# An attention and MLP-mixer kernel: sums transposed by TensorE, transposing DMAs two head pairs ahead, one store for 128 partitions, and another order in the first group's last token mixing

## The chip, the cores and the metric

The kernel runs on one core of one Trainium2 chip. The metric is the device time of one execution in microseconds (us). Before the change the median of three runs is 425.3 us (421.85 to 425.76).

## The reference, cut to what matters

The inputs are q, k and v of 8 batches, 12 heads, 448 positions and 64 elements a head, and four weight matrices. All is float32 outside; the kernel computes in fp16 with fp32 sums.

```python
scores = scale * q @ k.T - log(448)              # per batch and head, 448 x 448
attn   = 1 / (1 + exp(-scores))                  # a sigmoid, no softmax
x      = concat over heads of attn @ v           # 8 x 448 x 768
h      = relu(x.T @ w_tok1) @ w_tok2             # token mixing, 448 -> 256 -> 448
u      = x + h.T
h2     = relu(u @ w_ch1) @ w_ch2                 # channel mixing, 768 -> 1536 -> 768
out    = u + h2
```

## The kernel before, in words

The eight batches are four **groups** of two; the two batches of a group share the 128 partitions (64 each). A position is p * 7 + j, so a tile of 448 positions is seven blocks j of 64 partitions. Heads go in six **pairs** a group, 24 pairs in all, counted n = 6 * group + i.

Per pair, `load` (line 72) fetches k, q and v with six DMAs from the POOL queue, which turn fp32 into fp16. `turn` (line 96) makes kT and qT: in the first group TensorE transposes into PSUM and DVE copies out; later, DVE copies k and q into an order that suits (line 106, tiles kp and qp) and SP issues one transposing DMA each (line 109). `scores(i, j)` (line 135) makes four matmuls and a sigmoid on ACT; `values(i)` (line 158) makes 28 matmuls into xT; `back(i)` (line 180) turns xT into x_nat, by TensorE in the first group and by a transposing DMA later.

Token mixing is `tok1` (lines 202 to 217, tiles k1 and h1T) and `tok2(j)` (lines 219 to 250): DVE adds PSUM to x_nat and writes u in fp32, and then DVE or ACT casts u to u16 in fp16. `uturn(j)` (line 252) turns u16 into uT: in the first group TensorE transposes and DVE or ACT copies out, in the later groups SP issues a transposing DMA a block (line 255). Channel mixing is `ch1` (line 275: six matmuls of 512 or 384 columns, then a relu on DVE into h2aT) and `ch2` (line 293: twelve matmuls of 384 columns, then a DVE add into u), followed by `store(j)`: two DMAs from SP, one for each half of the partitions.

Nothing is scheduled by a planner: the order is the order in which the code is written. `first_attention` writes the first group's attention with the first two thirds of its token mixing between the rounds, and the last third (columns 512 to 768) behind it. `phase(grp, nxt)` then writes 38 units of the channel mixing of one group: 12 of `ch1` on blocks 0 to 3, 12 on blocks 4 to 6, and 14 of `ch2`. Among the first 30 it puts the attention of the next group in visits of three rounds, the first visit behind the second unit; among the last eight it puts that group's token mixing (`front1`, `front2`). PSUM has three double banks ("pair", used by scores, values and token mixing) and two single ones ("one"). Each engine takes its instructions in order, and so do the queues of SP and POOL.

In the trace and below, names lose part of their numbers: qk_1_0 in the second group is the score tile of pair i = 1 and block j = 0, c_0_6_0 is unit 6 of `ch1` of group 0 on blocks 0 to 3 (or a tile of `ch2`, where line 297 says so), xb is the tile of `back`, yn that of `tok2`, ut that of `uturn`, tk and tq those of `turn` in the first group.

## Time and profile before

| | |
|---|---|
| median of three runs | 425.3 us (421.85 to 425.76) |
| profiled execution | 417.46 us, of which the span is 415.7 us |
| PE busy | 372.6 us, 90% of the span, 3348 matmuls |
| DVE, ACT, POOL busy | 169.1, 190.3 and 92.9 us |
| chain that ended last | PE 70%, DMA 16%, DVE 7%, POOL 3% |
| mean granted TensorE clock | 0.97 |
| DMA, of the time of 16 engines | 39.9% POOL's queue, 38.0% SP's queue |

A share of busy time is a mean over stages. The groups are worked on one after the other: the first group's attention fills the span up to about 62 us, its last token mixing up to 72 us, and then come four phases that begin at about 72, 170, 267 and 356 us. Idle time of PE inside these stretches is what the views of waits and windows show. A matmul's own duration includes a part that overlaps the next one, so that a series is priced by its whole time or by the distance from start to start.

### The profile page before, as it was taken

How to read it: one execution, taken by the hardware profiler on the slowest of the kernel's cores; microseconds unless marked ns; L12 is line 12 of the kernel's file. 1: busy time of each engine (PE TensorE's matmuls, PEld its weight loads, DVE VectorE, ACT ScalarE, POOL GpSimd, SP SyncE). 2: the span in 40 equal slices, each digit the busy share in tenths (PEclk: the TensorE clock that was granted, in tenths of full speed). 3: DMA queues.
4: the chain of work that ended last, by engine and by line, in shares of the span. 5: the costliest groups of instructions: out<-in, count | busy, mean ns of one | idle time of the engine just before them, and what ended most of it. 6: DMA issues, size and time to landing. Idle time of an engine off the chain costs nothing.

```text
span 415.7 us, 8015 instructions
## 1 busy us (share of the span) xinstructions
PE 372.6 (90%) x3348; PEld 191.6 (46%) x3348; DVE 169.1 (41%) x310; ACT 190.3 (46%) x214; POOL 92.9 (22%) x159
## 2 busy tenths in 40 slices
PE   2988977949799999949799999979999999999995
PEld 1444544414355555414355455424555555446662
DVE  1258673313342117822432224843432118655231
ACT  2896834537676630246766821067778530000000
POOL 8796344321422200231513300030000000000000
PEclk9999997769999999978999999999999999999999
DMA  7999999993999944995999963792543517500233
GB/s 104 182 194 182 196 128 197 165 150 52 143 135 160 149 123 92 172 145 85 111 156 116 142 166 77 147 176 46 113 59 70 118 43 127 122 0 2 76 92 99
DMA packets 96532, 49.98 MB, mean 120 GB/s; under 512 B 70256, under 2 KB 92784, under 8 KB 96496
## 3 DMA queue, kind: packets, MB, share of 16 engines
q0 software_dynamic: 25104, 21.93, 39.9%
q1 hardware_dynamic: 71392, 27.54, 38.0%
q8 instruction: 26, 0.43, 0.5%
q14 instruction: 10, 0.08, 0.1%
HBM read 43.84 MB, written 11.01 MB: 132 GB/s over the span
## 4 chain that ended last, share of the span: by engine, by line
PE 70%; DMA 16%; DVE 7%; POOL 3%; issue 2%; ACT 1%; POOLq 0%
DMA q_1_500<-in_q_dram 3%; DMA qT_1295<-qp_1296 2%; DMA qT_2455<-qp_2456 2%; DMA qT_2691<-qp_2692 2%; DMA qT_1535<-qp_1536 2%; DMA qT_3611<-qp_3612 2%; DMA k_5_239<-in_k_dram 1%; DMA k_1_86<-in_k_dram 1%; DMA uT_4409<-u_3_3_4417 1%; PE c_0_0_0_1271 L278 1%; PE c_0_6_0_1424 L278 1%; PE c_1_6_0_2580 L278 1%; PE c_0_1_0_1279 L278 1%; PE c_2_2_1_4360 L297 0%; PE c_2_2_0_4332 L297 0%
## 5 line engine op out<-in xcount | busy, mean ns | idle before, releaser
L278 PEld LDWEIGHTS <-w_ch_t 128*128 128x128 f16 x576 | 54.8, 100 | 63.6 <-issue 20.7
L297 PEld LDWEIGHTS <-h2aT_1269 128*128 128x128 f16 x168 | 15.5, 98 | 13.0 <-issue 3.5
L297 PEld LDWEIGHTS <-h2aT_3589 128*128 128x128 f16 x168 | 15.5, 98 | 13.0 <-issue 3.5
L297 PEld LDWEIGHTS <-h2aT_2433 128*128 128x128 f16 x168 | 15.5, 98 | 13.0 <-issue 3.5
L297 PEld LDWEIGHTS <-h2aT_4692 128*128 128x128 f16 x168 | 16.4, 98 | 10.9
L234 PEld LDWEIGHTS <-w_tok_n 128*64 128x64 f16 x252 | 13.0, 111 | 13.0 <-issue 8.6
L206 PEld LDWEIGHTS <-w_tok_t 64*128 64x128 f16 x252 | 12.5, 97 | 9.5 <-issue 3.0
L150 ACT ACTIVATE attn_0_0_3625<-qk_0_0_3624,att_bias 128x896 f16<-128x896 f32 x1 | 1.0, 1007 | 18.4 <-PE qk_0_0_3624 L143 18.4
L86 POOL DMA_DIRECT2D k_5_3615<-in_k_dram x2 | 1.2, 602 | 36.0 <-DVE qp_3612 L106 36.0
L86 POOL DMA_DIRECT2D k_5_2459<-in_k_dram x2 | 1.2, 602 | 35.0 <-DVE qp_2456 L106 35.0
L150 ACT ACTIVATE attn_0_0_2469<-qk_0_0_2468,att_bias 128x896 f16<-128x896 f32 x1 | 1.0, 1007 | 17.4 <-PE qk_0_0_2468 L143 17.4
L117 PE MATMUL tk_135<-ident,k_0_72 128*64 128x128 f16 x14 | 1.0, 311 | 5.6 <-POOL ident masks.py:199 5.6
L143 PE MATMUL qk_1_0_2566<-qT_2455,kT_2451 64*64 64x448 f16 x4 | 0.6, 570 | 5.4 <-DMA qT_2455<-qp_2456 5.4
L143 PE MATMUL qk_1_0_1410<-qT_1295,kT_1291 64*64 64x448 f16 x4 | 0.6, 571 | 5.3 <-DMA qT_1295<-qp_1296 5.3
L150 ACT ACTIVATE attn_0_0_178<-qk_0_0_177,att_bias 128x896 f16<-128x896 f32 x1 | 1.0, 1007 | 7.0 <-PE qk_0_0_177 L143 7.0
L285 DVE TENSOR_SCALAR h2aT_1269<-c_0_6_0_1424 128x512 f16<-128x512 f32 x1 | 0.7, 692 | 8.0 <-PE c_0_6_0_1424 L278 8.0
L285 DVE TENSOR_SCALAR h2aT_2433<-c_1_6_0_2580 128x512 f16<-128x512 f32 x1 | 0.7, 692 | 7.9 <-PE c_1_6_0_2580 L278 7.9
L143 PEld LDWEIGHTS <-kT_2451 64*64 64x64 f16 x28 | 0.8, 113 | 6.7 <-issue 6.5
L143 PEld LDWEIGHTS <-kT_1291 64*64 64x64 f16 x28 | 0.8, 113 | 6.6 <-issue 6.4
L86 POOL DMA_DIRECT2D k_5_1299<-in_k_dram x2 | 1.2, 609 | 11.5 <-DVE qp_1296 L106 11.5
L117 PEld LDWEIGHTS <-k_0_72 128*64 128x64 f16 x14 | 0.8, 165 | 5.5 <-issue 5.5
L150 ACT ACTIVATE attn_1_0_2567<-qk_1_0_2566,att_bias 128x896 f16<-128x896 f32 x1 | 1.0, 1007 | 5.0 <-PE qk_1_0_2566 L143 5.0
(1244 smaller groups left out, 954.0 us busy)
## 6 DMA issues: line engine op xcount, KB each, us to landing
w_ch_t<-in_moe_w_ch_dram POOLq DMA_DIRECT2D x6, 768.0 KB, 11.8
w_tok_t<-in_moe_w_tok_dram POOLq DMA_DIRECT2D x2, 224.0 KB, 6.1
out_dram<-u_0_120 SPq DMA_DIRECT2D x2, 192.0 KB, 2.9
out_dram<-u_1_122 SPq DMA_DIRECT2D x2, 192.0 KB, 7.8
out_dram<-u_2_124 SPq DMA_DIRECT2D x2, 192.0 KB, 4.1
out_dram<-u_3_126 SPq DMA_DIRECT2D x2, 192.0 KB, 2.6
out_dram<-u_4_128 SPq DMA_DIRECT2D x2, 192.0 KB, 2.7
out_dram<-u_5_130 SPq DMA_DIRECT2D x2, 192.0 KB, 3.2
```

The costliest lines, as they stand in the source:

```text
L86: nc.gpsimd.dma_start(out=t[64 * b : 64 * b + 64, :, :, :], in_=src[2 * g + b, 2 * i : 2 * i + 2].rearrange("h (p j) e -> p h j e", j=J),)
L117: nc.tensor.transpose(out=ps[64 * h : 64 * h + 64, j, :, :], in_=raw[:, h, j, :], identity=ident[:, :],)
L143: nc.tensor.matmul(out=ps[64 * b : 64 * b + 64, h, 0:S], lhsT=kT[64 * h : 64 * h + 64, j, b, :], rhs=qT[64 * h : 64 * h + 64, :, b, :], st ...
L150: nc.scalar.activation(out=at[:, :, :], in_=ps[:, :, 0:S], func=SIGMOID, bias=bias_t[:, :], scale=att_scale,)
L206: nc.tensor.matmul(out=ps[:, b, 0 : c1 - c0], lhsT=w_tok1_t[64 * b : 64 * b + 64, j, 128 * tcb : 128 * tcb + 128], rhs=self.x_nat[64 * b : ...
L234: nc.tensor.matmul(out=d[64 * b : 64 * b + 64, :], lhsT=w_tok2_n[:, tcb, j, :], rhs=self.h1T[:, b, tcb, c0 + w * m : c0 + w * m + w], star ...
L278: nc.tensor.matmul(out=ps[:, :, :], lhsT=w_ch1_t[:, db, 128 * cb : 128 * cb + 128], rhs=self.uT[:, db, j0:j1, :], start=(db == 0), stop=(d ...
L285: nc.vector.tensor_scalar(out=self.h2aT[:, cb, j0:j1, :], in0=ps[:, :, :], scalar1=0.0, scalar2=None, op0=MAX,)
L297: nc.tensor.matmul(out=ps[:, :], lhsT=self.h2aT[:, cb, j, :], rhs=w_ch2_t[:, cb, c], start=(cb == 0), stop=(cb == NCB - 1),)
```

## The change

1. **Two pairs ahead.** `turn(n)` for the pairs of the later groups is called at round (i, 3) for pair i + 2, where before it was round (i, 0) for pair i + 1. The second group's first two pairs are turned behind the first group's last `tok2` and before the third unit of the phase. `load` is now called through `load_to`, three pairs ahead of a turn and not four, v has seven buffers in place of six, `w_ch1` is loaded some rounds later, and the identity is made before the first loads.
2. **Sums transposed by TensorE.** `uturn` of the later groups makes six transposes a block on TensorE into a double bank, two blocks at a time, and ACT copies them out. The `front2` calls come one unit earlier, with the transposes one or two units behind them and the last block's behind the next phase's first unit.
3. **128-partition stores.** One DMA a block in place of two.
4. **fp16 sums first.** `tok2_late` in the first group's last token mixing lets DVE write u16 straight from PSUM; `rest` makes the same adds into the fp32 sums later. In the first phase the first two relus go to ACT.

```diff
     def load(n):
-        if n >= NG * NP:
-            return
...
-                bufs=6 if what == "v" else 8,
+                bufs=7 if what == "v" else 8,
...
         if "q" in whats:
-            load(n + 4)
+            load_to(n + 3)
...
-        def uturn(self, j, d0=0, d1=6, eng=None):
-            u16 = self.u16s[j]
-            if not self.first:
-                nc.sync.dma_start_transpose(out=self.uT[:, :, j, :], in_=u16[:, :])
-                return
-            ps = bank(f"ut_{self.g}_{j}_{d0}", [128, NDB, 128], FP16)
...
+        def tok2_late(self, js, c0, c1):
...
+            for m, j in enumerate(js):
+                nc.vector.tensor_tensor(
+                    out=self.u16s[j][:, c0:c1],
+                    in0=self.x_nat[:, j, c0:c1],
+                    in1=ps[:, m, 0:w],
+                    op=ADD,
+                )
+            def rest():
...
+            return rest
+        def uturn(self, j, d0=0, d1=6, eng=nc.scalar, nj=1):
+            n = d1 - d0
+            name = f"ut_{self.g}_{j}_{d0}"
+            if n == NDB:
+                ps = pp.tile([128, 2, 8, 128], FP16, tag="pair", bufs=3, name=name)
+            else:
+                ps = bank(name, [128, nj, n, 128], FP16)
+            for m in range(nj):
+                for db in range(n):
+                    c = 128 * (d0 + db)
+                    nc.tensor.transpose(
+                        out=ps[:, m, db, :],
+                        in_=self.u16s[j + m][:, c : c + 128],
+                        identity=ident[:, :],
+                    )
...
         def store(self, j):
-            for b in range(2):
-                nc.sync.dma_start(
-                    out=out[2 * self.g + b].rearrange("(p j) d -> p j d", j=J)[:, j, :],
-                    in_=self.us[j][64 * b : 64 * b + 64, :],
-                )
+            rows = out.rearrange("b (p j) d -> (b p) j d", j=J)
+            nc.sync.dma_start(
+                out=rows[128 * self.g : 128 * self.g + 128, j, :], in_=self.us[j][:, :]
+            )
...
-        if j == 0 and (i == NP - 1 or not grp.first):
-            turn(grp.g * NP + i + 1)
+        if j == 3 and not grp.first:
+            turn(grp.g * NP + i + 2)
...
-        for j in range(J):
-            grp.tok2(j, *cols, nc.scalar)
-            if j >= 2:
-                grp.uturn(j - 2, 4, 6, nc.scalar)
+        late = [grp.tok2_late(js, *cols) for js in ((0, 1), (2, 3))]
+        grp.uturn(0, 4, 6, nc.scalar, 2)
+        late.append(grp.tok2_late((4, 5), *cols))
+        grp.uturn(2, 4, 6, nc.scalar, 2)
+        late[0]()
+        grp.tok2_late((6,), *cols)()
+        turn(NP)
+        for f in late[1:]:
+            f()
...
+            if grp.first and f is units[2][1]:
+                turn(NP + 1)
             f()
...
-            4: lambda: front2((0, 1)),
-            5: lambda: front2((2, 3)),
-            6: lambda: front2((4, 5)),
-            7: lambda: front2((6,)),
+            3: lambda: front2((0, 1)),
+            4: lambda: front2((2, 3)),
+            5: lambda: (nxt.uturn(0, nj=2), front2((4, 5))),
+            6: lambda: (nxt.uturn(2, nj=2), front2((6,))),
+            7: lambda: nxt.uturn(4, nj=2),
```

The first place where the order moves is DVE at the end of the first group's last token mixing (u_0_0 to u_0_6 are the fp16 sums, u_0 to u_6 the fp32 ones, kp and qp the copies of `turn`). Before:

```order
L215 TENSOR_SCALAR h1T_118<-k_0_1_512_1184 128x2x256
L241 TENSOR_TENSOR u_0_120<-x_nat_117,yn_0_512_1200 128x256
L241 TENSOR_TENSOR u_6_132<-x_nat_117,yn_6_512_1258 128x256
L285 TENSOR_SCALAR h2aT_1269<-c_0_0_0_1271 128x512
L285 TENSOR_SCALAR h2aT_1269<-c_0_1_0_1279 128x512
L106 COPY kp_1292<-k_1_497 128x2x7x64
L106 COPY qp_1296<-q_1_500 128x2x7x64
```

The rows for u_1 to u_5 are left out there. After:

```order
L220 TENSOR_SCALAR h1T_118<-k_0_1_512_1158 128x2x256
L273 TENSOR_TENSOR u_0_0_121<-x_nat_117,yl_0_1174 128x256
L273 TENSOR_TENSOR u_0_5_131<-x_nat_117,yl_4_1202 128x256
L282 TENSOR_TENSOR u_0_120<-x_nat_117,yl_0_1174 128x256
L282 TENSOR_TENSOR u_1_122<-x_nat_117,yl_0_1174 128x256
L273 TENSOR_TENSOR u_0_6_133<-x_nat_117,yl_6_1221 128x256
L282 TENSOR_TENSOR u_6_132<-x_nat_117,yl_6_1221 128x256
L111 COPY kp_1229<-k_0_485 128x2x7x64
L111 COPY qp_1233<-q_0_488 128x2x7x64
```

The rows for blocks 1 to 4 are left out. Ten adds now stand between the relu of h1T and the copies of the second group's pair 0, and those copies, which stood in round (5, 0) of the first group's attention before, now stand here.

The second place is the queue of SP at the end of the second group's token mixing and the start of the third group's attention. Before:

```order
L309 DMA out_dram<-u_5_130 64x768 x2
L255 DMA_TRANSPOSE uT_2150<-u_1_5_2162 128x6x128
L309 DMA out_dram<-u_6_132 64x768 x2
L255 DMA_TRANSPOSE uT_2150<-u_1_6_2164 128x6x128
L109 DMA_TRANSPOSE kT_2451<-kp_2452 128x7x128
L109 DMA_TRANSPOSE qT_2455<-qp_2456 128x7x128
```

After:

```order
L350 DMA out_dram<-u_5_130 128x768
L350 DMA out_dram<-u_6_132 128x768
L114 DMA_TRANSPOSE kT_2523<-kp_2524 128x7x128
L114 DMA_TRANSPOSE qT_2527<-qp_2528 128x7x128
```

All seven transposing DMAs of the sums are gone. kT_2451 is the third group's pair 1 and kT_2523 is its pair 2: pairs 0 and 1 were issued in the group before.

## Rows read from the trace of the kernel before

**Rows 1.** The page: the TensorE clock granted, in 40 slices of the span.

```profile
PEclk9999997769999999978999999999999999999999
```

**Rows 2.** What PE waited for: us in total, times, longest us.

```profile
PE qk_1_0_2566 L143 <- DMA qT_2455<-qp_2456: 5.4, 1, 5.4
PE qk_1_0_1410 L143 <- DMA qT_1295<-qp_1296: 5.3, 1, 5.3
PE qk_3_0_2834 L143 <- DMA qT_2691<-qp_2692: 3.1, 1, 3.1
PE qk_3_0_1678 L143 <- DMA qT_1535<-qp_1536: 2.6, 1, 2.6
PE qk_1_0_3713 L143 <- DMA qT_3611<-qp_3612: 2.5, 1, 2.5
PE c_2_0_0_3591 L278 <- DVE u_6_2163 L305: 1.0, 1, 1.0
PE tk_192 L117 <- DMA k_1_86<-in_k_dram: 0.9, 1, 0.9
...
PE c_3_0_0_4693 L278 <- DMA uT_4409<-u_3_3_4417: 0.5, 1, 0.5
```

**Rows 3.** Windows: stretch, us, busy of PE, PEld, DVE, ACT, POOL, clock, DMA, GB/s.

```profile
72.10:77.30 5.20, 5.18 (x18) 1.92 (x21) 0.74 (x2) 0.69 (x2) 0.00 (x0) 0.54 1.16 210
...
89.90:95.00 5.10, 5.10 (x20) 1.63 (x20) 0.69 (x1) 1.90 (x2) 0.00 (x0) 0.60 1.09 139
```

**Rows 4.** The chain that ended last, second group's attention: start us, us, what.

```profile
90.81 2.68 PE c_0_6_0_1424 L278 x6
...
96.91 1.40 PE c_0_8_0_1486 L278 x6
```

**Rows 5.** Timeline, last token mixing and first visit: start us, us, engine, what.

```profile
65.48 0.69 DVE L215 TENSOR_SCALAR h1T_118<-k_0_1_512_1184 128x512 f16<-128x512 f32 x1 [2.80 <-PE k_0_1_512_1184 L206]
...
66.69 0.42 DVE L241 TENSOR_TENSOR u_0_120<-x_nat_117,yn_0_512_1200 128x256 f32<-128x256 f16 x1 [0.52 <-PE yn_0_512_1200 L234]
67.03 0.42 DVE L241 TENSOR_TENSOR u_1_122<-x_nat_117,yn_1_512_1207 128x256 f32<-128x256 f16 x1
...
72.12 2.72 PE L278 MATMUL c_0_0_0_1271<-uT_119,w_ch_t 128*128 128x512 f16 x6
...
77.26 0.38 PE L143 MATMUL qk_0_0_1308<-qT_930,kT_926 64*64 64x448 f16 x4
...
77.86 0.38 DVE L106 COPY kp_1292<-k_1_497 128x896 f16<-128x896 f16 x1
...
78.34 1.23 SPq L109 DMA_TRANSPOSE kT_1291<-kp_1292  x1
```

**Rows 6.** DMA issues: what, queue, count, us from issue to landing.

```profile
qT_1295<-qp_1296 SPq DMA_TRANSPOSE x1, 10.1
...
qT_3133<-qp_3134 SPq DMA_TRANSPOSE x1, 8.2
...
qT_3611<-qp_3612 SPq DMA_TRANSPOSE x1, 7.1
...
qT_3709<-qp_3710 SPq DMA_TRANSPOSE x1, 2.9
```

**Rows 7.** Timeline: seven transposes of 128 columns on TensorE, in `back`.

```profile
61.46 0.55 PE L189 MATMUL xb_5_1159<-ident,xT_5_1138 128*128 128x128 f16 x7
```

**Rows 8.** Line 189, the same transposes: duration ns min/median/max, first and last start.

```profile
L189 PE MATMUL xb_5_1159<-ident,xT_5_1138 x7: 216/218/219, 61.5 to 61.8; 128*128 128x128 f16 x7
```

**Rows 9.** Timeline of SP's queue at the end: the last store's two issues.

```profile
411.26 1.10 SPq L309 DMA_DIRECT2D out_dram<-u_6_4422  x2
```

**Rows 10.** DMA view: queues (packets, MB, share), issues of channel weights, us to landing.

```profile
q0 software_dynamic: 25104, 21.93, 39.9%
q1 hardware_dynamic: 71392, 27.54, 38.0%
...
w_ch_t<-in_moe_w_ch_dram POOLq DMA_DIRECT2D x6, 768.0 KB, 11.8
```

More of the change, by code (lines that the diff above doesn't have):

```diff
@@ L70, with load_to @@
     heads = {}
+    loaded = []
+    def load_to(last):
+        while len(loaded) <= min(last, NG * NP - 1):
+            load(len(loaded))
+            loaded.append(True)
     def load(n):
-        if n >= NG * NP:
-            return
         g, i = divmod(n, NP)
@@ L250, in tok2 @@
                 eng.tensor_copy(out=u16[:, c0:c1], in_=u[:, c0:c1])
-        def uturn(self, j, d0=0, d1=6, eng=None):
-            u16 = self.u16s[j]
-            if not self.first:
-                nc.sync.dma_start_transpose(out=self.uT[:, :, j, :], in_=u16[:, :])
-                return
-            ps = bank(f"ut_{self.g}_{j}_{d0}", [128, NDB, 128], FP16)
-            for db in range(d0, d1):
-                nc.tensor.transpose(
-                    out=ps[:, db, :],
-                    in_=u16[:, 128 * db : 128 * db + 128],
-                    identity=ident[:, :],
-                )
-            dst, src = self.uT[:, d0:d1, j, :], ps[:, d0:d1, :]
+        def tok2_late(self, js, c0, c1):
+            w = c1 - c0
+            name = f"yl_{self.g}_{js[0]}"
+            ps = pair_bank(name) if len(js) > 1 else bank(name, [128, 1, w])
+            for m, j in enumerate(js):
+                for tcb in range(2):
+                    for b in range(2):
+                        nc.tensor.matmul(
+                            out=ps[64 * b : 64 * b + 64, m, 0:w],
+                            lhsT=w_tok2_n[:, tcb, j, :],
+                            rhs=self.h1T[:, b, tcb, c0:c1],
+                            start=(tcb == 0),
+                            stop=(tcb == 1),
+                        )
+            for m, j in enumerate(js):
+                nc.vector.tensor_tensor(
[3 more added lines that the diff above has]
+                    op=ADD,
+                )
+            def rest():
+                for m, j in enumerate(js):
+                    nc.vector.tensor_tensor(
+                        out=self.us[j][:, c0:c1],
+                        in0=self.x_nat[:, j, c0:c1],
+                        in1=ps[:, m, 0:w],
+                        op=ADD,
+                    )
+            return rest
@@ L273, in start_channel, with ch1 @@
             )
-        def ch1(self, cb, j0, j1):
+        def ch1(self, cb, j0, j1, eng=nc.vector):
             ps = bank(f"c1_{self.g}_{cb}_{j0}", [128, j1 - j0, 128])
@@ L284, in ch1 @@
                 )
-            nc.vector.tensor_scalar(
-                out=self.h2aT[:, cb, j0:j1, :],
-                in0=ps[:, :, :],
-                scalar1=0.0,
-                scalar2=None,
-                op0=MAX,
-            )
+            dst = self.h2aT[:, cb, j0:j1, :]
+            if eng is nc.vector:
+                eng.tensor_scalar(out=dst, in0=ps[:, :, :], scalar1=0.0, scalar2=None, op0=MAX)
+            else:
+                eng.activation(out=dst, in_=ps[:, :, :], func=RELU)
         def ch2(self, j, half):
@@ L381, in unit @@
             def unit(cb=cb):
-                grp.ch1(cb, 0, JA)
-                if grp.first and cb in (1, 3):
-                    grp.uturn(J - 2 + cb // 2, 4, 6, nc.scalar)
+                grp.ch1(cb, 0, JA, nc.scalar if grp.first and cb < 2 else nc.vector)
+                if grp.first and cb == 0:
+                    grp.uturn(4, 4, 6, nc.scalar, 2)
+                if grp.first and cb == 1:
+                    grp.uturn(6, 4, 6, nc.scalar)
+                if not grp.first and cb == 0:
+                    grp.uturn(6)
             units.append((1.3, unit))
@@ L423, in front2 @@
                 nxt.tok2(j, 0, D, nc.vector)
-            for j in js:
-                nxt.uturn(j)
         fronts = {
@@ L478 @@
     with tc.manual_schedule():
-        load(0)
         make_identity(nc, ident)
         nc.vector.memset(bias_t[:, :], att_bias)
-        load(1)
-        load(2)
+        load_to(2)
         load_tok1()
         load_tok2()
-        load(3)
+        load_to(3)
         groups = [Group(g) for g in range(NG)] + [None]
```

6 lines of the change are left out of this document (4 added, 2 removed).

## The prediction

> **What bounds the kernel now.** I read the granted clock first [rows 1], then what PE waited for, then windows around the waits, then the chain, the timeline and the DMA view. PE is busy for 90% of the span by the table of the profile, so the question is which of its idle stretches go, and what is added to it. The list of PE's waits [rows 2] is short: five waits for a qT that a transposing DMA brings, in the second group's attention (5.3 and 2.6 us), the third's (5.4 and 3.1) and the fourth's (2.5), and small ones at the start of a channel mixing (1.0 and 0.5). The reader is to see that all five are for q, the second DMA of its pair, and that they stand at pairs 1 and 3.
>
> The longest waits have a tail. Behind the 5.3 us wait the stretch from 89.9 to 95.0 us runs at a mean granted clock of 0.60 [rows 3], that is mostly at 1.2 GHz and not 2.4, and c_0_6_0 takes 2.68 us where c_0_8_0 takes 1.40 [rows 4]. With part of the unit and the scores beside it I put this tail at 1.8 us. The clock's line dips again at the third group's 5.4 us wait [rows 1], so the tail counts twice; at the waits of 2.5 to 3.1 us there is no dip. A third dip lies at the end of the first group's token mixing: 72.1 to 77.3 us runs at 0.54 [rows 3].
>
> **The change, part by part.**
>
> *Two pairs ahead, where it holds.* From pair 0's first scores at 77.26 [rows 5] to c_0_6_0 at 90.81 [rows 4], just behind pair 1's first, lie seven rounds and the 5.3 us wait, so seven rounds without a wait take 8 us. That was the lead of a turn at (i, 0) for pair i + 1. What it has to cover: from the copy's start to SP's issue of k 0.48 us (77.86 to 78.34), the issue 1.23 [rows 5], and q's landing. The thirteen q that have loads beside them land 7.1 to 10.1 us after their issue, with 8.2 in the middle [rows 6]. Together 9 to 12 us, more than 8: this is why PE waits. A turn at (i, 3) for pair i + 2 has 11 rounds, 13 us by the same rate, and covers the worst of them. So all five waits go: second group 5.3 + 1.8 + 2.6 = 9.7, third 5.4 + 1.8 + 3.1 = 10.3, fourth 2.5. The two at the start of a channel mixing go as well, since DVE starts a unit earlier there and no DMA brings the sums: 1.0 + 0.5. What is late next is PE's own work.
>
> *Where it doesn't hold.* Pair 0 of the second group is turned no longer in round (5, 0) but behind the last token mixing, while its scores still stand right behind the second unit of `ch1`. This is a new wait. The relu of h1T ends at 66.17 and the first add started at 66.69 [rows 5]; now that add waits for two blocks' matmuls, so 67.1. Ten adds stand ahead of the copies, one every 0.34 us (66.69 to 67.03 [rows 5]), and I estimate 0.6 us of waits for PE between them: 71.1. Then 0.48 to k's issue, 71.6, and 1.28 to q's, 72.9; with 8.2 us to land, 81.1. I take the middle of the rows with loads beside them, since the next pair's load waits for just these copies and starts with them. PE is ready sooner: its first scores ran at 77.26 behind a stretch at 1.2 GHz [rows 3, 5], and nothing ahead of them gets longer, so it stands 3.8 us or more, and the scores run 81.1 - 77.26 = +3.8 later. The bounds: with the fourth group's landing, 2.9 us [rows 6], q is there at 75.8, PE's own work decides, and it is about -1; with 10.1 it is +5.7. Behind such a wait I expect the slow tail too: +1.5 (bounds 0 and 1.8). Behind PE stand ACT's sigmoids and DVE's relus of the next units; the fp32 sums and pair 1's copies are ahead of them in DVE's order and are done.
>
> *Transposes on TensorE.* Three groups by seven blocks by six make 126 new matmuls with their weight loads, all on the path. Seven of the kind take 0.55 us [rows 7], and each alone lasts 0.219 [rows 8], so they start 0.055 apart. A burst of twelve takes 12 x 0.055 and up to 0.16 more, where what follows starts anew; with half of that 0.74, and a burst of six 0.41. Three of the first and one of the second a group make 2.6, three groups +7.9. Bounds 6.9 (126 x 0.055) and 27.6 (126 x 0.219, no overlap); I take the first row's value, a burst too. ACT, which copies out, has no other work there, and each burst reads sums that were cast a unit earlier, so the copies cost nothing under the unit of `ch2` behind them; were that cover too short, the next phase's first unit would wait, under 2 us a group.
>
> *The rest.* The last store has one issue in place of two that take 1.10 us together [rows 9]: -0.5 (0 to -0.6). Two DVE copies of 0.38 us leave the first group's attention: -0.3 (0 to -0.7). The identity ahead of the loads makes the first q some 0.6 us later; behind that PE waits 0.9 us for pair 1's k [rows 2], which is issued when it was, and hides it: 0 (to +0.6). Loading one pair later, with `w_ch2` ahead of two pairs on POOL, moves no wait of PE that I see; it should have those weights, which take 11.8 us to land [rows 10], out of the way when pair 0 is turned. The seventh buffer for v lets POOL run on: 0.
>
> **The sum**, against the profiled execution's own 417.46 us: -0.3 + 3.8 + 1.5 - 9.7 - 10.3 - 2.5 - 1.5 + 7.9 - 0.5 = -11.6, so 405.9. The median of the runs shown is 7.8 us above the profiled execution, and no view says why. I carry the difference over: 425.3 - 11.6 = **413.7**.
>
> **The rivals.**
>
> *The new wait is short.* If the DMAs are empty when pair 0 is turned, q lands in 2.9 us [rows 6], PE hardly stands and the clock does not fall: 4.8 + 1.5 less, 407.4. For it speaks that `w_ch2` is out of the way, against it that the next load starts with the copies. Chance 0.2.
>
> *The waits come back.* POOL's queue fills 39.9% and SP's 38.0% of the DMAs over the span [rows 10], and loads lie in the first three groups only. If transposes and loads take longer a pair than PE does, an earlier turn only stands longer in the queue. If half of the 22.5 us of waits and tails stays, it is 425.0, no change. Against it: without loads q lands in 2.9 us, and 21 transposes leave the queue. It decides if q takes over 11 us from its issue. Chance 0.15.
>
> *Slower: transposes do not overlap.* If each costs its full 0.219 us, since every one needs its own weights, the 126 cost 27.6 and not 7.9: 433.4. It decides from 0.155 us each, where all of the gain is eaten. Against it stands the burst of seven in 0.55 us [rows 7]. Chance 0.07. The Trainium skill has a rule on this side ("TensorE: Matmul & The Clock Gate", Part 4: PE-mode transpose): a transpose of 128 by 128 took about 275 ns within a kernel, and does not count as activity for the clock. By its figure, which is an estimate here, 126 would cost 34.7 us and the sum would be 440.5; the trace of before speaks against it with 0.55 us for seven.
>
> *The change does not do what it says* for pair 0 of the second group alone, and that is in the forecast.
>
> The forecast has 0.55, and 0.03 are left for what I do not see. The measurement tells 1% apart, about 4 us: faster is under 421.0. The forecast and the short wait are faster nearly whole, with a little of the third case: 0.78. Within 1% are most of the third case and the forecast's edge, 0.14; slower 0.08. The range runs from 404, the short wait with part of the unexplained 7.8 us gone, to 421, the forecast with the worst landing and half of one group's waits left.
>
> **What would show it.** Right: no wait for qT at pairs 1 and 3 of any group; one wait of 4 to 9 us at qk_0_0 of the second group, with a dip of the clock behind it; bursts of twelve transposes in 0.7 to 0.9 us; the second to fourth token mixings each longer by 2 to 3 us. Wrong: waits for qT at later pairs, a first unit of `ch1` that waits for ACT, or transposes from 0.1 us up.

## The result, and the profile after

The changed kernel takes 403.62 us (median of four runs, 400.88 to 404.65) where the kernel before took 425.31 (421.85 to 425.76): ratio 0.961, 95% interval 0.949 to 0.974. This ratio, like those below, compares only the runs within 1.5% of each kernel's fastest; the ratio of the medians is 0.949, since the kernel before also has slower runs (its 33 runs beside the experiments below go from 415.46 us at a mean granted clock of 0.978 to 433.06 us at 0.948). The gain is 21.7 us by the medians and about 16 us (3.9%) by the ratio. The changed kernel's profiled execution takes 403.25 us with a span of 401.5, so profile to profile the gain is 14.2 us, and another 7.5 are in the medians alone.

The page of the changed kernel, the granted clock in 40 slices; one dip is left of the three in [rows 1]:

```profile
PEclk9999999779999999999999999999999999999999
```

What PE waited for in the changed kernel (us in total, times, longest us), the three longest of the list:

```profile
PE qk_0_0_1277 L148 <- DMA qT_1232<-qp_1233: 7.5, 1, 7.5
PE tk_135 L122 <- DMA k_0_77<-in_k_dram: 5.2, 1, 5.2
PE tq_152 L122 <- DMA q_0_80<-in_q_dram: 1.3, 1, 1.3
```

The five waits for qT of [rows 2] are gone, and the two at the start of a channel mixing with them. One new wait for qT has come, at pair 0 of the second group. The two waits for the first loads stand at the very start of the span. They have a counterpart before, which [rows 2] leaves out: there the first transposes waited 5.6 us for the identity, in the page's words

```profile
L117 PE MATMUL tk_135<-ident,k_0_72 128*64 128x128 f16 x14 | 1.0, 311 | 5.6 <-POOL ident masks.py:199 5.6
```

The timeline around it (start us, us, engine, line, what; in brackets how long the engine had stood idle and for what), the counterpart of [rows 5]:

```profile
64.87 0.42 DVE L273 TENSOR_TENSOR u_0_0_121<-x_nat_117,yl_0_1174 128x256 f16<-128x256 f16 x1 [0.61 <-PE yl_0_1174 L265]
...
67.54 1.46 PE L321 MATMUL c_0_0_0_1251<-uT_119,w_ch_t 128*128 128x512 f16 x6 [0.35 <-ACT uT_119 L311]
...
68.56 0.39 DVE L111 COPY kp_1229<-k_0_485 128x896 f16<-128x896 f16 x1
...
69.03 1.33 SPq L114 DMA_TRANSPOSE kT_1228<-kp_1229  x1
...
69.24 0.59 POOL L91 DMA_DIRECT2D k_4_1306<-in_k_dram  x1 [7.38 <-DVE qp_1233 L111]
...
70.42 1.31 SPq L114 DMA_TRANSPOSE qT_1232<-qp_1233  x1
...
78.72 0.59 PE L148 MATMUL qk_0_0_1277<-qT_1232,kT_1228 64*64 64x448 f16 x4 [7.48 <-DMA qT_1232<-qp_1233]
...
79.99 2.74 PE L321 MATMUL c_0_2_0_1315<-uT_119,w_ch_t 128*128 128x512 f16 x6
```

The first unit of `ch1` starts at 67.54 and runs at full speed (1.46 us, 2.72 before). Then PE stands 7.48 us, and c_0_2_0 behind the wait takes 2.74. The row of POOL is the one to remember: the load of K for pair 4 is issued 0.2 us after the transposing DMA of pair 0's K, and what it had waited for is pair 0's copies, which free the raw tiles.

Windows of the changed kernel over the same place (stretch, us, busy of PE, PEld, DVE, ACT, POOL, clock, DMA, GB/s): first units, wait, and what follows, as [rows 3] before:

```profile
67.50:71.20 3.70, 3.20 (x18) 1.52 (x17) 3.37 (x11) 1.12 (x3) 1.52 (x3) 1.00 1.36 189
71.20:78.70 7.50, 0.04 (x1) 0.12 (x1) 0.39 (x1) 0.84 (x2) 4.54 (x8) 0.73 1.38 134
78.70:83.50 4.80, 4.78 (x21) 1.70 (x21) 0.69 (x1) 2.80 (x3) 1.19 (x2) 0.50 1.30 173
```

Behind the wait PE runs 4.8 us at 0.50, so at 1.2 GHz throughout, and loses 2.4 us. Before, a stretch of nearly the same length was slow ahead of pair 0's scores [rows 3].

DMA issues of the changed kernel (what, queue, count, us to landing), and SP's queue, beside [rows 6, 10]:

```profile
qT_1232<-qp_1233 SPq DMA_TRANSPOSE x1, 8.3
...
qT_1302<-qp_1303 SPq DMA_TRANSPOSE x1, 13.1
...
qT_3235<-qp_3236 SPq DMA_TRANSPOSE x1, 10.4
...
qT_3719<-qp_3720 SPq DMA_TRANSPOSE x1, 2.9
```

```profile
q1 hardware_dynamic: 54144, 23.41, 31.4%
```

q still takes 5.1 to 10.4 us from issue to landing where loads run beside it, and 13.1 once, at pair 1 of the second group. The lead hides the others; pair 1's q, issued at 75.65, is there at 88.75, and PE starts that pair's scores at 88.87. SP's queue is emptier, 31.4% for 38.0%, and its transposes are hardly faster for it.

The new transposes on PE in the timeline of the second group's token mixing, as [rows 7] before, and their duration (ns min/median/max, first and last start) beside [rows 8]:

```profile
158.23 0.50 PE L301 MATMUL ut_0_0_2356<-ident,u_1_0_2148 128*128 128x128 f16 x6
158.57 0.50 PE L301 MATMUL ut_0_0_2356<-ident,u_1_1_2150 128*128 128x128 f16 x6
159.00 0.84 PE L239 MATMUL yn_4_0_2370<-h1T_2145,w_tok_n 128*64 128x384 f16 x8
```

```profile
L301 PE MATMUL ut_0_0_2356<-ident,u_1_0_2148 x6: 219/219/219, 158.2 to 158.5; 128*128 128x128 f16 x6
```

Each lasts 0.219 us, but twelve take 159.00 - 158.23 = 0.77 us of PE's path, 0.064 each.

The last store in SP's queue is one issue where [rows 9] show two in 1.10 us:

```profile
397.83 0.33 SPq L350 DMA_DIRECT2D out_dram<-u_6_4482  x1
```

All runs can be laid side by side by stages. A stage ends where PE starts the first `ch1` matmul or the first `tok1` matmul of a group in the timeline; us in the profiled execution:

| kernel | to ch1 of group 1 | to tok1 of 2 | to ch1 of 2 | to tok1 of 3 | to ch1 of 3 | to tok1 of 4 | to ch1 of 4 | to the end |
|---|---|---|---|---|---|---|---|---|
| before | 72.1 | 74.2 | 24.0 | 72.1 | 25.0 | 64.1 | 24.6 | 59.8 |
| before, second profile | 72.3 | 82.6 | 24.5 | 74.1 | 24.7 | 67.5 | 24.4 | 59.7 |
| changed | 67.5 | 73.0 | 26.0 | 61.7 | 26.3 | 61.7 | 26.0 | 59.3 |
| sums by DMA | 69.6 | 73.2 | 24.0 | 61.4 | 24.6 | 61.3 | 24.4 | 58.8 |
| lead only | 71.4 | 71.0 | 24.9 | 61.3 | 25.0 | 61.3 | 24.7 | 59.7 |
| no lead | 70.0 | 73.9 | 26.0 | 72.2 | 26.0 | 66.6 | 26.0 | 59.3 |
| fastest (below) | 70.3 | 62.3 | 24.1 | 61.4 | 24.2 | 61.3 | 24.0 | 59.2 |

The second, fourth and sixth column hold attention beside channel mixing. In the changed kernel the fourth and sixth stand at 61.7, and the second is still 11 us longer: the new wait is most of it.

### The profile page after: what moved, and what is told of

The parts are those of the page before. It is cut to its first block, busy times and chain, and to the rows that moved or that the text cites. A ratio compares the mean times of both kernels' runs of the same rounds, so it can differ in the third digit from the quotient of the medians.

```text
span 401.5 us, 8197 instructions
## 1 busy us (share of the span) xinstructions
PE 371.5 (93%) x3474; PEld 196.9 (49%) x3474; DVE 170.1 (42%) x315; ACT 203.4 (51%) x218; POOL 93.3 (23%) x159
## 3 DMA queue, kind: packets, MB, share of 16 engines
q1 hardware_dynamic: 54144, 23.41, 31.4%
## 4 chain that ended last, share of the span: by engine, by line
PE 83%; DMA 9%; POOL 4%; DVE 2%; issue 1%; POOLq 0%; DVEq 0%
DMA k_3_1236<-in_k_dram 3%; DMA qT_1232<-qp_1233 2%; DMA w_tok_s<-in_moe_w_tok_dram 2%; DMA k_2_95<-in_k_dram 1%; DMA k_5_353<-in_k_dram 1%; PE c_0_2_0_1315 L321 1%; PE c_0_3_0_1323 L321 1%; PE c_2_4_1_4591 L338 1%; PE c_2_2_1_4421 L338 1%; PE c_2_2_0_4393 L338 1%; PE c_2_1_1_4332 L338 1%; PE c_2_0_1_4261 L338 1%; PE c_1_2_1_3290 L338 1%; PE c_1_2_0_3262 L338 1%; PE c_1_1_1_3184 L338 1%
## 5 line engine op out<-in xcount | busy, mean ns | idle before, releaser
L321 PEld LDWEIGHTS <-w_ch_t 128*128 128x128 f16 x576 | 53.9, 99 | 58.4 <-issue 14.3
L239 PEld LDWEIGHTS <-w_tok_n 128*64 128x64 f16 x224 | 11.4, 109 | 9.6 <-issue 4.8
L91 POOL DMA_DIRECT2D k_0_2661<-in_k_dram x2 | 1.2, 604 | 38.9 <-DVE qp_2528 L111 38.9
L311 ACT ACTIVATE uT_3338<-ut_0_0_3548 128x1536 f16<-128x1536 f16 x1 | 1.5, 1451 | 8.9 <-PE ut_0_0_3548 L301 8.9
L311 ACT ACTIVATE uT_2146<-ut_0_0_2356 128x1536 f16<-128x1536 f16 x1 | 1.5, 1451 | 8.9 <-PE ut_0_0_2356 L301 8.9
L311 ACT ACTIVATE uT_4469<-ut_0_0_4679 128x1536 f16<-128x1536 f16 x1 | 1.4, 1450 | 8.9 <-PE ut_0_0_4679 L301 8.9
L155 ACT ACTIVATE attn_0_0_169<-qk_0_0_168,att_bias 128x896 f16<-128x896 f32 x1 | 1.0, 1007 | 7.5 <-PE qk_0_0_168 L148 7.5
L155 ACT ACTIVATE attn_0_0_1278<-qk_0_0_1277,att_bias 128x896 f16<-128x896 f32 x1 | 1.0, 1007 | 7.4 <-PE qk_0_0_1277 L148 7.4
L222 ACT ACTIVATE h1T_3337<-k_2_0_384_3428 128x768 f16<-128x768 f32 x1 | 0.8, 810 | 4.7 <-PE k_2_0_384_3428 L211 4.7
L91 POOL DMA_DIRECT2D k_4_1306<-in_k_dram x2 | 1.3, 658 | 7.8 <-DVE qp_1233 L111 7.4
L222 ACT ACTIVATE h1T_2145<-k_1_0_384_2236 128x768 f16<-128x768 f32 x1 | 0.8, 811 | 4.4 <-PE k_1_0_384_2236 L211 4.4
```

The source lines that it names most:

```text
L91: nc.gpsimd.dma_start(out=t[64 * b : 64 * b + 64, :, :, :], in_=src[2 * g + b, 2 * i : 2 * i + 2].rearrange("h (p j) e -> p h j e", j=J),)
L155: nc.scalar.activation(out=at[:, :, :], in_=ps[:, :, 0:S], func=SIGMOID, bias=bias_t[:, :], scale=att_scale,)
L222: eng.activation(out=dst, in_=src, func=RELU)
L239: nc.tensor.matmul(out=d[64 * b : 64 * b + 64, :], lhsT=w_tok2_n[:, tcb, j, :], rhs=self.h1T[:, b, tcb, c0 + w * m : c0 + w * m + w], star ...
L311: eng.activation(out=dst, in_=src, func=COPYF)
L321: nc.tensor.matmul(out=ps[:, :, :], lhsT=w_ch1_t[:, db, 128 * cb : 128 * cb + 128], rhs=self.uT[:, db, j0:j1, :], start=(db == 0), stop=(d ...
```

## The experiments

All times are medians, with the lowest and highest run; ratios are to the kernel before on the same chip, with their 95% interval. Two chips were used, on which the kernel before has medians of 424.2 to 425.6 us.

**1. The kernel before, profiled again.** No edit.

> The kernel before, unchanged, looked at once more: its timed runs have their median 7.8 us above its profiled execution. Theory: the excess stands at the same places as the waits of the profiled execution (TensorE waits for qT of groups 2 to 4, 22.3 us in that profile, with slow-clock stretches behind them), because how long a transfer takes in a full queue differs from one execution to the next; then a profile with a time of 421 to 426 us shows 26 to 32 us of such waits, and the stretches from the start of a group's channel mixing to its second phase and the token mixings stay within 0.5 us of the first profile. Rival: the excess is spread over TensorE's work (a lower granted clock, or a slower start); then the waits for qT stay at 21 to 23 us and the spans of the phases outside them grow. If this execution too takes about 417 us, neither is told apart.

Measured: 431.59 us, the span 429.8, mean granted clock 0.941 (0.970 in the first profile). Its page's busy and clock lines and its waits for qT:

```profile
PE 380.2 (88%) x3348; PEld 193.2 (45%) x3348; DVE 169.4 (39%) x310; ACT 190.5 (44%) x214; POOL 93.5 (22%) x159
...
PEclk9899996968979999997969999996999999999998
```

```profile
PE qk L143 <- DMA qT<-qp: 24.8, 5, 10.1
```

Windows of this execution: the longest wait, and behind it.

```profile
83.40:93.90 10.50, 0.41 (x6) 0.14 (x5) 1.39 (x3) 1.01 (x1) 2.39 (x4) 0.76 1.47 131
93.90:100.00 6.10, 6.10 (x28) 2.10 (x32) 0.95 (x2) 1.91 (x2) 0.00 (x0) 0.57 1.08 85
```

The same five waits, 24.8 us in place of 18.9, the one at pair 1 of the second group 10.1 in place of 5.3. By the table of stages 13.9 of the 14.1 us between the two executions lie in the three stages with attention (8.5, 2.0 and 3.4); the others stay within 0.6. So the theory was right about the place. It was wrong about the size: it had 26 to 32 us of waits in an execution of 421 to 426 us, and the 22.3 us that it names for the first profile are 18.9 in the view. The waits are 5.9 of the 14.1 us. PE's busy time, 380.2 us for 372.6 with the same 3348 matmuls by the two pages, is another 7.6, and the granted clock is lower (0.941 for 0.970). So the rival was right about the larger part, but that part lies in the stages with the waits and is not spread over the span. This is one execution, longer than any of the four timed runs of the result. That the median runs of the kernel before hold such waits and such a clock, and that its profiled execution of 417.46 us was a lucky one, is inferred from it and not shown.

**2. Sums by transposing DMA again**, all else as in the changed kernel.

```diff
+            if not self.first:
+                nc.sync.dma_start_transpose(out=self.uT[:, :, j, :], in_=self.u16s[j][:, :])
+                return
...
-            5: lambda: (nxt.uturn(0, nj=2), front2((4, 5))),
...
```

> The changed kernel with one part undone: the sums of groups 2 to 4 are transposed by transposing DMAs again (21 DMAs return to SP's queue, 126 transposes leave TensorE), the lead of two pairs stays. Theory (the TensorE transposes cost 2.0 to 2.4 us in each of three groups, 7.1 us in all, and buy little, since a lead of two pairs hides the transfers either way): 396 to 400 us beside 403.6 of the changed kernel, token mixings of groups 2 to 4 back to 45.6, 46.6 and 46.2 us, waits for qT at the later pairs under 1 us each. Rival (the 21 transposing DMAs were what delayed q, so that taking them out is what makes the lead suffice): waits for qT of 3 us and more return at the pairs whose q is issued behind them, and the time is 406 to 412 us.

Measured: 397.73 us (397.04 to 398.99), ratio 0.941 (0.933 to 0.949), 5.9 us under the changed kernel. The theory holds: the token mixings of groups 2 to 4 are back at 24.0, 24.6 and 24.4 us, and of the waits for the sums little returns:

```profile
PE qk L148 <- DMA qT<-qp: 8.0, 1, 8.0
...
PE c L324 <- DMA uT<-u: 0.9, 2, 0.6
```

So the TensorE transposes cost more than they save.

**3. The lead alone, on the kernel before.**

```diff
-        if j == 0 and (i == NP - 1 or not grp.first):
-            turn(grp.g * NP + i + 1)
+        if j == 0 and i == NP - 1 and grp.first:
+            turn(NP)
+        if j == 3 and not grp.first:
+            turn(grp.g * NP + i + 2)
...
+            if grp.first and f is units[0][1]:
+                turn(NP + 1)
```

The loads follow as in the change, `w_ch1` is issued at (2, 4), v has seven buffers, and the identity comes first; none of these four was run by itself.

> The kernel before with one part alone: K and Q are turned two pairs ahead and loads follow the turn; the sums still go by transposing DMAs, pair 0 of group 2 is still turned in the first group's attention, the last token mixing of the first group and the two-half stores are as before. Theory (the lead takes away the waits at pairs 1 and 3 and the slow clock behind them, which were 22.5 us of the profiled 417.5, and nothing new comes in): 394 to 400 us, so faster than the changed kernel, with no wait for qT above 2 us after the first pair of group 2. Rival (without the other parts the lead doesn't hold, since the SP queue is as full as before): 408 to 415 us with waits for qT of 3 us or more.

Measured: 400.83 us (399.59 to 401.10), ratio 0.948 (0.942 to 0.955). One wait for qT of 4.5 us is left, at pair 1 of the second group, none elsewhere. The first channel mixing units of the later groups wait 2.4 us for their sums, 1.5 before. From the page (in each row the idle time before the group, and what ended most of it):

```profile
L283 PE MATMUL c<-uT,w_ch_t 128*128 128x512 f16 (+1 forms) x576 | 119.7, 362 | 2.5 <-DMA uT<-u 2.4
...
L148 PE MATMUL qk<-qT,kT 64*64 64x448 f16 x672 | 52.5, 372 | 7.2 <-DMA qT<-qp 4.5
```

This is slower than the theory's bound by 0.8 us, and its "no wait for qT above 2 us after the first pair" fell; but the lead alone brings all of the gain of the changed kernel. By the medians it brings 2.8 us more, though the two ranges of runs touch.

**4. The lead undone in the changed kernel.**

```diff
-        if j == 3 and not grp.first:
-            turn(grp.g * NP + i + 2)
+        if j == 0 and not grp.first:
+            turn(grp.g * NP + i + 1)
...
-            load_to(n + 3)
+            load_to(n + 4)
```

> The changed kernel with the lead undone: from group 2 on, K and Q are turned one pair ahead again (at the first round of the pair before), with the loads four pairs behind; the sums stay on TensorE, the last token mixing and the stores as in the changed kernel. Theory (the lead is what takes the waits away): waits for qT of 2.5 us and more at pairs 1 and 3 of the groups, 16 to 25 us in all, with the slow clock behind them, 415 to 425 us. Rival (21 sums fewer in SP's queue and one store instead of two are enough): no wait for qT beyond the first pair's above 1 us, 402 to 408 us.

Measured: 421.94 us (418.37 to 427.96), ratio 0.994 (0.988 to 0.999); five waits for qT, the longest of them at pair 0 of the second group, which is still turned late:

```profile
PE qk L148 <- DMA qT<-qp: 18.8, 5, 7.3
```

The theory holds: without the lead the other parts together bring 3 us by the medians, and 0.1 to 1.2% by the ratio.

**5. Pair 0 of group 2 turned early**, in round (5, 0) of the first group's attention, and pair 1 where pair 0 was.

```diff
+        if j == 0 and i == NP - 1 and grp.first:
+            turn(NP)
...
-        turn(NP)
+        turn(NP + 1)
...
-            if grp.first and f is units[2][1]:
-                turn(NP + 1)
```

> The changed kernel with pair 0 of group 2 turned early: in round (5,0) of the first group's attention, where the kernel before had it, and pair 1 at the place behind the last token mixing where the change put pair 0. Theory (the 7.5 us wait at qk_0_0 and the slow clock behind it, about 2 us, come only from turning pair 0 so late): 394 to 397 us, with at most 1 us of wait at qk_0_0 and the clock at 1.0 there. Rival (pair 1, turned where pair 0 was, is late in its turn: its K and Q land 8 to 13 us after issue and its first scores come about 9 us after pair 0's): a wait of 3 to 5 us at qk_0_1 or before it, and 399 to 402 us.

Measured: 404.64 us (400.29 to 405.07), ratio 0.956 (0.947 to 0.964), no faster than the changed kernel. The theory fell. The timeline of PE: pair 0's scores without a wait, and then pair 1's.

```profile
72.69 0.76 PE L148 MATMUL qk<-qT,kT 64*64 64x448 f16 x12
...
87.83 0.96 PE L148 MATMUL qk<-qT,kT 64*64 64x448 f16 x8 [7.98 <-DMA qT<-qp]
88.72 4.95 PE L321 MATMUL c<-uT,w_ch_t 128*128 128x512 f16 x12
```

The rival's mechanism was right and its 3 to 5 us too small: the wait went to the next pair undiminished. In the changed kernel the 7.5 us at pair 0 had covered pair 1's landing of 13.1.

**6. Both pairs early**, on the kernel of run 2: pair 0 as in run 5, pair 1 right behind the last x_nat transposes.

```diff
         grp.back(NP - 1)
+        turn(NP + 1)
         cols = (2 * third, D)
...
-        turn(NP)
```

> Sums by transposing DMA (as in the run that undid the TensorE transposes, 397.7 us), and both first pairs of group 2 turned within the first group: pair 0 in round (5,0) of its attention, pair 1 right behind the last x_nat transposes, ahead of the last token mixing. Theory (the one wait that is left, 8.0 us for the q of whichever pair is turned last before the channel mixing, and the slow clock behind it, about 2.9 us by c at 5.05 us for 12 matmuls where full speed takes 2.76, both come from issuing that pair's transposes less than 10 us ahead of its scores; the two VectorE copies that come back into the first attention cost 1.2): 397.7 - 8.0 - 2.9 + 1.2 = 388 us, 386 to 391, no wait for qT above 1 us. Rival (the next pair in line, pair 2, becomes late as pair 1 did when pair 0 alone was turned early): a wait of 3 to 8 us two visits later, and 393 to 398 us.

Measured: 401.39 us (399.76 to 402.67), ratio 0.949 (0.942 to 0.957), worse than both bounds. The waits for qT are two, 2.70 us at pair 1 and 5.05 at pair 3:

```profile
83.24 0.57 PE L148 MATMUL qk<-qT,kT 64*64 64x448 f16 x8 [2.70 <-DMA qT<-qp]
83.75 4.45 PE L324 MATMUL c<-uT,w_ch_t 128*128 128x512 f16 x12
...
107.33 0.59 PE L148 MATMUL qk<-qT,kT 64*64 64x448 f16 x4 [5.05 <-DMA qT<-qp]
```

So turning early is not enough: pair 1's q takes 18.5 us to land. With the turns the loads had moved too, since each follows the tile that a turn frees: `w_ch2` is issued at 62.2 us (52.9 in the changed kernel), just ahead of pair 1's transposes at 63.3. That the weight is what delayed this q is likely, and was not run by itself.

**7. The second channel weight loaded late.**

```diff
-        at(5, 1, load_ch2)
...
+            if grp.first and f is units[8][1]:
+                load_ch2()
```

> The changed kernel with one move: the load of the second channel weight (three transfers of 768 KB) is issued ahead of the ninth unit of the first channel mixing instead of in the first group's attention. Theory (those 2.3 MB move while pair 0's K and Q of group 2 are transposed, and share the DMA engines with them, so q needs 8.3 us to land where an unhindered one takes 2.9): q lands in 4 to 6 us, the wait at qk_0_0 falls from 7.5 to 3 to 5 us, 399 to 402 us. Rival (the loads of the later pairs move up into the place of the weight and hinder the transposes as much): q lands in 7 to 9 us, wait 7 to 8 us, 402 to 405 us. If the weight is now late for the second phase, a wait for w_ch_t shows at its first matmul, at about 119 us.

Measured: 418.87 us (418.01 to 419.37), ratio 0.990 (0.983 to 0.996). The theory fell at pair 0: it waits 8.2 us with the weight out of the way, as the rival said. And a second wait, which neither expected, came where the weight now is: it is issued at 90.5 us, behind it the q of pair 3 takes 15.8 us to land, for which PE waits 11.85, and a transposing DMA of x_nat takes 7.93 us to issue in SP's queue.

```profile
105.57 7.93 SPq L188 DMA_TRANSPOSE x_nat<-xT  x1
```

```profile
118.36 0.59 PE L148 MATMUL qk<-qT,kT 64*64 64x448 f16 x4 [11.85 <-DMA qT<-qp]
```

**8. The old last token mixing in the changed kernel.**

```diff
+        for j in range(J):
+            grp.tok2(j, *cols, nc.scalar)
+            if j >= 2:
+                grp.uturn(j - 2, 4, 6, nc.scalar)
         turn(NP)
...
-                grp.ch1(cb, 0, JA, nc.scalar if grp.first and cb < 2 else nc.vector)
+                grp.ch1(cb, 0, JA)
```

> The changed kernel with the first group's last token mixing as before: sums in fp32 first, cast to fp16 by ScalarE, transposed one token block at a time, the first two units' results on VectorE; pair 0 of group 2 still turned behind it. Theory (the mixing ends 2.5 to 4 us later, pair 0's copies come that much later, and the rest moves along): first channel matmul at about 71 us instead of 67.5 to 69.6, wait at qk_0_0 still 7 to 8 us, 406 to 408 us. Rival (when q lands is set by the loads that the DMA engines carry, and not by when the copy is made): the wait shrinks by as much as the mixing ends later, 403 to 405 us.

Measured: 405.79 us (404.59 to 406.97), ratio 0.959 (0.952 to 0.965). Between the two: from the last `tok1` to the first `ch1` the mixing takes 7.9 us in place of 5.7, and the wait behind it is 5.8 us in place of 7.5. Most of what the fp16 sums gain, the wait takes back.

**9 and 10. Loads held until q has landed**, on the changed kernel, and on that of run 2.

```diff
         if "q" in whats:
             load_to(n + 3)
+            if n >= NP:
+                nc.gpsimd.tensor_copy(out=held[:, :], in_=turned[(n, "q")][:, 0, 0, 0:1])
```

> The changed kernel with the loads of K, Q and V held back: behind each pair's turn from group 2 on, GpSimd copies one element per partition of the transposed Q, so that the load of the pair four ahead, which so far starts the moment the raw tile is free, is issued only when that Q has landed. Theory (q of pair 0 takes 8.3 us because the loads of pair 4 and 5, 672 KB each, are issued between 69.2 and 76 us, in the 9 us in which the transposes are on their way; moving the weight alone left the landing at its length for that reason): q lands in 3 to 5 us, the wait at qk_0_0 is 3 to 4.5 us, 398 to 401 us. Rival (K's and Q's transposes, one behind the other in SP's queue, need these 8 us by themselves when they come together with stores, or the engines are held by something else): q lands in 7 to 9 us, wait 7 to 8, 402 to 405 us.

> The kernel with the sums by transposing DMA and the lead of two pairs (397.7 us), with the same hold of the loads as in the run above. Theory: the wait of 8.0 us for the first q falls to 3 to 4.5 us and the rest stays: 393 to 395 us. Rival (nothing in the loads delays it): 397 to 399 us. If the loads that are held come too late for pairs further on, waits for k or q at the copies (VectorE on in_q_dram) and for qT appear there, and the time is over 398 us.

Measured on the changed kernel: 402.99 us (400.67 to 403.50). SP, PE and POOL in its timeline:

```profile
73.28 1.29 SPq L115 DMA_TRANSPOSE qT<-qp  x1
...
76.65 0.76 PE L151 MATMUL qk<-qT,kT 64*64 64x448 f16 x12 [2.55 <-DMA qT<-qp]
76.66 0.19 POOL L132 COPY held<-qT 128x1 f16<-128x1 f16 x1 [12.02 <-DMA qT<-qp]
...
77.34 4.45 PE L324 MATMUL c<-uT,w_ch_t 128*128 128x512 f16 x12
```

q is there 3.4 us after its issue in place of 8.3, and PE waits 2.5 us in place of 7.5: the mechanism is shown. The stage falls from 73.0 to 66.7 us. The median, however, fell by 0.6 us only, outside the theory; in this profiled execution, the fastest of its five, the first `ch1` was 2.9 us later than in the changed kernel's and the third group's token mixing 0.9 longer. The 2.9 us are scatter: the profiled executions of runs 2, 9 and 10 and of the changed kernel, whose order is the same up to there, reach the first `ch1` at 67.5 to 70.4 us. Why the other four runs keep so little of the 6.3 us stays open. On the kernel of run 2 the same edit gives 394.18 us (392.42 to 395.30) for 397.73, as its theory had it. Its waits:

```profile
PE qk L151 <- DMA qT<-qp: 2.4, 1, 2.4
...
PE k L214 <- DMA x_nat<-xT: 1.3, 1, 1.3
```

The hold has a price: the token mixings of groups 2 and 3 take 24.9 and 25.7 us where run 2 has 24.0 and 24.6, and a wait of 1.3 us for a transpose of x_nat stands in the second of them.

**11. Pair 0 by TensorE, pair 1 by DMA with the loads held, sums by DMA.**

```diff
-            if n >= NP:
+            if n > NP:
                 perm = pa.tile(...)
...
         grp.back(NP - 1)
+        turn(NP)
...
-        turn(NP)
+        turn(NP + 1)
...
-            if grp.first and f is units[2][1]:
-                turn(NP + 1)
```

The hold is that of the runs above, from pair 1 on and ahead of `load_to`.

> Sums by transposing DMA; pair 0 of group 2 is transposed by TensorE (28 transposes and two copies out of PSUM by VectorE, as for the pairs of the first group) right behind the last x_nat transposes, pair 1 by DMA where pair 0 was, with the loads held until its Q and each later one has landed. Theory (the wait of 8.0 us and its slow clock, about 2.9 us, are the price of the DMA way for a pair that is turned less than 10 us ahead; TensorE does it in about 2 us, part of them in a gap of 0.7 us): 397.7 - 8.0 - 2.9 + 1.5 = 388 us, 386 to 391, no wait for qT above 1 us. Rival (pair 1 is late then, as in the run that turned pair 0 alone early, 8.0 us): 396 to 400 us. In between, at 391 to 396 us, pair 1 or a later pair waits 2 to 5 us.

Measured: 387.86 us (387.11 to 391.39), the fastest here: 15.8 us under the changed kernel, 36.7 under the median of the kernel before beside it (424.52) and 27.6 under that kernel's fastest run there (415.46). The theory holds to 0.2 us. Its clock line, and its timeline of PE:

```profile
PEclk9999999999999999999999999999999999999999
```

```profile
63.30 0.58 PE L123 MATMUL tk<-ident,k 128*64 128x128 f16 x14
64.08 0.58 PE L123 MATMUL tq<-ident,q 128*64 128x128 f16 x14 [0.20 <-DVE x_nat L200]
...
73.95 0.76 PE L151 MATMUL qk<-qT,kT 64*64 64x448 f16 x12
74.64 2.76 PE L327 MATMUL c<-uT,w_ch_t 128*128 128x512 f16 x12
```

No dip of the clock, no wait for qT. The stage of the second group's attention is 62.3 us, within 1 of the others.

**12. The same without the hold.** The copy of run 9 taken out of it.

> The best kernel so far (387.9 us: sums by DMA, pair 0 of group 2 by TensorE, loads held until the Q turned before has landed) without the hold: a pair's load starts again as soon as its raw tile is free. Theory (the loads of the pairs ahead are what makes a transposing DMA late, and pair 1, turned at about 71.5 us and first used at about 84, is caught by them as in the run that turned pair 0 alone early, where its q took up to 15.8 us): a wait of 4 to 8 us at pair 1 and slow clock behind it, 393 to 398 us. Rival (TensorE's turn of pair 0 was all that was needed, and pair 1 has 10 us to spare): no wait above 1 us, 386 to 389 us.

Measured: 394.67 us (390.39 to 397.40), ratio 0.938 (0.913 to 0.964), 6.8 us over run 11 by the medians; the ranges of runs touch (run 11 goes up to 391.39), and the two are from different chips. The stage of the second group's attention is 70.3 us, 8.0 longer. The time is the theory's, the place only in part: 1.85 us at pair 1, then 0.94 and 3.17 at the two pairs behind it, 6.0 in all. The last of them, and what follows it:

```profile
102.65 0.38 PE L148 MATMUL qk<-qT,kT 64*64 64x448 f16 x4 [3.17 <-DMA qT<-qp]
102.96 4.78 PE L324 MATMUL c<-uT,w_ch_t 128*128 128x384 f16 x18
```

## Why the prediction was right, and where its size was off

It said 413.7 with a range of 404 to 421, and faster; measured were 403.62, 0.4 us under the range's low end, and the profile has the gain at the places named. That the range nearly reaches it is luck in part: its low end was built on a short wait, which did not come. By its own steps, from profile to profile (-14.2 where the sum had -11.6):

- **The lead.** Right, to 0.5 us: the stages with the third and fourth group's attention fell by 10.4 and 2.4 us with a burst of six transposes (0.33) added to each, so the lead brings 10.8 and 2.7 (10.3 and 2.5 forecast). The first two stages fell by 5.7 with 1.5 and 2.4 added by the new wait and its tail (below), so it brings 9.6 there (9.7). Run 3 shows it alone, run 4 the rest without it. The two waits at the start of a channel mixing are gone too: the third and fourth group's token mixings before are 1.0 and 0.6 us longer than the second's, which has no such wait (1.5 forecast together).
- **The new wait.** Right in place, cause and landing (8.3 us, 8.2 taken from the middle of [rows 6]; "the thirteen q" leave out a fourteenth with loads beside it, pair 0's own in the kernel before, which took 10.5). On the path it came to +1.5 us (pair 0's scores at 78.72 for 77.26) and not +3.8. Of the difference 1.9 is no effect of the change: this execution reached the last token mixing 0.9 us earlier, and ran its `tok1` in 1.70 us where the profiled execution of before took 2.71; the kernel before took 1.70 as well in run 1. How early this stretch is reached scatters: the first `tok1` starts at 28.1 us in the changed kernel and at 28.1 to 30.1 in runs 2 to 12, at 29.0 and 29.8 in the kernel before. The tail was 2.4 us, not 1.5.
- **The two copies that leave the first group.** -0.3 forecast, 0.0 measured: from the first `tok1` to the last one's start it is 33.76 us in both kernels. With the identity ahead of the loads the first scores start at 8.4 to 9.6 us (the changed kernel and runs 2 to 12, 9.1 in the middle) for 8.5 and 8.6 before, about the 0.6 us expected; in the first `tok1` this is lost in the scatter named above.
- **The transposes on TensorE.** +7.9 forecast. Against the token mixings of run 12, which have no waits in them (24.0 us each), those of the changed kernel are 2.0, 2.3 and 2.0 longer; with three bursts of six that is 7.4. Against the kernel before the mixings are 2.0, 1.3 and 1.4 us longer, where the forecast's signs had 2 to 3, since those of before hold the two waits. What the transposes take away is small: run 2 has 0.9 us of waits for sums, run 3 2.4. The sign "a first unit of `ch1` that waits for ACT" came only in the first channel mixing, where PE waits 0.3 us for ACT's copy and 0.5 for its relu, and in no later group. The third rival, 0.219 us each, is refuted by 0.77 for twelve. The Trainium skill ("TensorE: Matmul & The Clock Gate", Part 4) gives about 275 ns for one within a kernel; here one lasts 219 ns, and its price in a burst is 64 ns. What that passage says of the clock no run here tests.
- **The last store.** -0.5 forecast with a bound of -0.6, -0.8 measured: from its issue to the end of the span it is 3.7 us where it was 4.4. Runs 2 and 3 differ by 1.0 in their last stage.
- **The step with the wrong size** is the last of the sum: "The median of the runs shown is 7.8 us above the profiled execution, and no view says why. I carry the difference over". Carrying it over took it for work that the change does not touch. Run 1 has the excess of one longer execution in the stages with the waits for qT: 24.8 us of waits and 380.2 us of busy PE at 431.59 us, 18.9 and 372.6 at 417.46. The changed kernel, with none of the five waits and one new one, has its profiled execution (403.25) amid its runs. So the 7.8 most likely went with the waits and the slow clock behind them: 417.46 - 11.6 = 405.9, the sum before that step, is 2.3 us from what was measured.

The rival of the short wait (407.4) had the nearer number for the wrong reason: its q was to land in 2.9 us, and it took 8.3. The rival "the waits come back" named 11 us as the landing from which it decides; only pair 1 of the second group went over that, with 13.1, and pair 0's wait had covered it by 0.1 us (75.65 + 13.1 for scores at 88.87). Run 5, without pair 0's wait, shows it in the open.

What makes q late where loads run: not the 21 sums in SP's queue (with them back, run 2, the rest does not wait), not the weight alone (run 7), but what POOL loads while a transpose is under way; at pair 0 that begins with the load which its own copies let go. Held back, q of pair 0 lands in 3.4 us (run 9). Over all q the hold does less: the middle landing goes from 7.4 us in the changed kernel to 5.1 in run 9, the longest from 13.1 to 9.2. The rule that fits stands in the Trainium skill ("DMA: Bandwidth & Descriptors", Queues, rings and completion order): each DMA engine goes round the queues it has work for, packet by packet. By that rule a transpose in an emptier queue still shares with every load. The landings agree: 2.9 us in the fourth group, 3.4 with the loads held, 8.3 with them.

## What to carry to other kernels

Where timed runs lie above the profiled one, look at a second profile before carrying the difference over: if it sits in the waits that the change removes, expect it to go with them. Ask of each buffer what its release starts; here the copy that feeds an urgent transpose frees the tile whose reload slows that transpose, and holding that load until the transpose had landed was worth 3.6 us (run 10) and 6.8 (run 12) between medians, each pair from two chips on which the kernel before differs by 0.4 and 1.1. Turning one pair earlier only moved such a wait to a later pair (runs 5 and 6), and the short lead was better served by TensorE, with 28 transposes in 1.2 us of PE, than by DMA: run 11 is 6.3 us under run 10.

## What was not expected of the hardware

The clock behind a wait does not follow the wait's length alone: behind 2.5 to 3.1 us [rows 2] no dip shows in the clock's line of the kernel before, behind 1.85 in run 12 neither, but behind 2.55 in run 9 and 2.70 in run 6 twelve `ch1` matmuls take 4.45 us each time, and 2.76 at full speed, and behind 3.17 in run 12 eighteen take 4.78 us. In run 9 the clock falls behind the wait and not in it: the twelve score matmuls right behind it still run at full speed (0.76 us), and the windows show it (the clock is the third number from the end of each row):

```profile
69.00:77.00 8.00, 4.64 (x42) 2.48 (x40) 4.84 (x15) 3.01 (x6) 0.19 (x1) 1.00 1.07 167
77.00:82.00 5.00, 5.00 (x31) 1.72 (x24) 0.86 (x2) 2.80 (x3) 4.85 (x10) 0.66 0.93 133
```

The same 28 matmuls of the last `tok1`, behind the same gaps of 0.8, 0.4 and 0.7 us, took 1.70 us in five executions and 2.5 to 2.9 in seven; the kernel before did both (2.71 and 1.70). With a weight load of 2.3 MB and the loads of the pairs on the way, one transposing DMA took 7.93 us to issue in SP's queue (run 7) and another 7.03 (run 6), where the shortest issues take 1.22.
